# Stages 2 to 4 of an attention and two-layer kernel in five blocks of 924 tokens, not six of 768

## The chip, the core and the metric

The kernel runs on one NeuronCore of a Trainium2 chip. TensorE does the matrix products, VectorE and ScalarE prepare operands and take results away, GpSimd (POOL) helps in the first stage, and every transfer between HBM and SBUF is issued by SyncE (SP), one queue in program order. The metric is the device time of one execution in microseconds; lower is better.

## The reference

Inputs are fp32. An attention through 32 memory slots (8 batches, 8 heads, 576 tokens, width 64) is followed by two layers over all 4608 tokens:

```
attn_out = _attn_ref(**attn_kwargs)                       # [8, 8, 576, 64]
x = attn_out.transpose(0, 2, 1, 3).reshape(4608, 512)
r = np.maximum(x @ w_in, 0.0)                             # moe:  512 -> 2048
x = (s * (r * r) + b) @ w_out                             #       2048 -> 512
h = x @ w_in2                                             # moe2: 512 -> 2048
g = h * (1.0 / (1.0 + np.exp(-1.702 * h)))
y = g @ w_out2                                            #       2048 -> 512
```

## The kernel before

There are four stages. Stage 1 is the attention with `w_in` and the relu, batch by batch; it writes `r` to HBM. Stage 2 is `r*r @ w_out` (weights `wo`), stage 3 `x @ w_in2` with its gating (`w1`), stage 4 `g @ w_out2` (`w2`). Between stages the data go through HBM (`r`, `x`, `g`).

**Blocks and products.** Stages 2 to 4 go over the tokens in `N` = 6 blocks of 2 x `TS` = 768. Each block's product is done in the manner of Strassen with seven half-size products instead of eight, numbered 1 to 7, on sums and differences of the halves of the operands; the tokens are halved too, so a matmul has `TS` = 384 columns. Each operand is split into a high part (`oh`) and a low part (`ol`) that the fast fp32 format holds, and each product of operands is three matmuls: high by high, high by low, low by high (lines 885 to 887 and 1013 to 1015). One product on one quarter of the 2048-wide dimension is a group of 12 matmuls, and a block has 7 x 4 = 28 groups. PSUM tiles `X`, `Y` and `Z` collect them.

**Preparing operands.** `down` (stages 2 and 4) loads for each quarter five tiles `A`, `B`, `D`, `C`, `E` (line 856); in stage 2 ScalarE squares them (line 858). Product 6 needs three subtractions on VectorE in a row, `A-B`, `D-B` and `D-A` (lines 865 to 867), then ScalarE (or VectorE) makes the high part (`hi`) and VectorE the low part (`lo`). `up` (stage 3) loads four `x` tiles per block and makes 14 operand tiles that are used by all four quarters. `leave` and `gate` take results out of PSUM and send them to HBM.

**Weights.** The weights of the seven products are prepared during the stage before (`prepare`) and written to HBM, each as high and low part side by side, 512 KB. `weights` loads 28 of them once at the start of a stage, where they stay. In stage 2 the quarters 0 to 2 are loaded as 256 KB and split at the start; quarter 3 (`kept`) is split in stage 1 and stays in SBUF.

**Slots.** SBUF tiles come from two pools of equal slots (line 192): 30 of 4 KB per partition for weights (`w`), 31 of 3 KB for everything else (`t`). A tile can be loaded when an earlier one of its pool has been read for the last time.

**The order.** Nothing is ordered by loops. Every step is recorded with a due time, the engines that can do it with an estimated cost, and what it reads and writes. `Order.sort` then takes one step after the other, by due time among those that can start, and hands out the slots of a pool in the order of due times. `B2` = 58.5 is the planned length of a block, from which all due times of stages 2 to 4 follow. The result is one fixed order per engine.

## Time and profile before

| | |
|---|---|
| median of the runs | 1363.14 us (1362.56 to 1363.47) |
| span of the profiled execution | 1361.4 us |
| TensorE busy (PE) | 1348.1 us, 99% |
| VectorE busy (DVE) | 1035.4 us, 76% |
| ScalarE busy (ACT) | 806.5 us, 59% |
| moved by DMA | 336.73 MB, mean 247 GB/s |

The profile gives the span from the first to the last instruction of one execution; its whole time is not given beside it, and the median of the runs lies 1.7 us above the span. Stage 1 takes the first 317 us; stages 2, 3 and 4 follow with borders near 658 and 996 us. Matmuls overlap one another, so their busy time is longer than the distance at which they start, and that distance is what counts. SP's column in order of time shows when a transfer was issued; the view of DMA issues shows how long it took to land.

### The profile page before, as it was taken

Reading aid. Unit: us, or ns where it says so; the run is one execution under the profiler, and the core shown is the slowest. Engines: PE = TensorE matmul, PEld = TensorE weight load, DVE = VectorE, ACT = ScalarE, POOL = GpSimd, SP = SyncE. Lnnn points to the kernel's source line nnn. Section 1 sums busy time; section 2 is a strip of 40 time slices with the busy share of each in tenths; the row PEclk is TensorE's granted clock in tenths of the full one; section 3 lists DMA queues with packets and bytes.
Section 4 is the critical chain, followed back from the end, with each engine's and each line's share of the span. In section 5 each row is a group of like instructions: output and inputs, shape, how many; then the busy total and the mean of one; then the engine's idle time right before and its main releaser. Section 6 shows DMA issues by size and latency. Waiting matters only on the chain.

```text
span 1361.4 us, 23704 instructions
## 1 busy us (share of the span) xinstructions
PE 1348.1 (99%) x9184; PEld 1306.9 (96%) x9184; DVE 1035.4 (76%) x1384; ACT 806.5 (59%) x1104; POOL 52.2 (4%) x42
## 2 busy tenths in 40 slices
PE   7999999999999999999999999999999999999998
PEld 5798888899999999999999999999999999999998
DVE  6878996899988898998756856665376776968682
ACT  5766666789777787777545554645443444434351
POOL 2201220200000000000000000000000000000000
PEclk8999999999999999999999999999999999999999
DMA  9989999797755775599876666576996544355541
GB/s 365 366 295 349 364 344 327 260 325 245 277 185 174 235 259 162 193 362 339 314 274 248 248 237 228 209 259 238 315 339 212 183 162 163 128 174 160 196 131 48
DMA packets 126400, 336.73 MB, mean 247 GB/s; under 512 B 14288, under 2 KB 14544, under 8 KB 126288
## 3 DMA queue, kind: packets, MB, share of 16 engines
q1 hardware_dynamic: 126288, 335.22, 70.6%
q8 instruction: 72, 1.18, 0.4%
q14 instruction: 40, 0.33, 0.1%
HBM read 205.93 MB, written 129.24 MB: 246 GB/s over the span
## 4 chain that ended last, share of the span: by engine, by line
PE 94%; DVE 4%; DMA 2%; issue 0%; ACT 0%; SPq 0%; ACTq 0%
PE X L885 10%; PE X L886 10%; PE X L887 10%; PE Y L885 5%; PE X L1014 5%; PE X L1015 5%; PE Y L886 5%; PE X L1013 5%; PE Y L887 5%; PE h L294 4%; PE h L296 4%; PE h L295 4%; PE Y L1014 2%; PE Y L1015 2%; PE Y L1013 2%; PE Z L885 2%
## 5 line engine op out<-in xcount | busy, mean ns | idle before, releaser
L294 PE MATMUL h<-ah,mh 128*128 128x288 f32 x512 | 155.3, 303 | 0.2
L270 DVE TENSOR_TENSOR u<-Y,u 128x768 f32<-128x768 f32 x60 | 57.4, 957 | 125.6 <-ACT u L1021 56.0
L296 PE MATMUL h<-ah,ml 128*128 128x288 f32 x512 | 151.4, 296 | 0.1
L295 PE MATMUL h<-al,mh 128*128 128x288 f32 x512 | 150.9, 295 | 0.0
L885 PE MATMUL X<-oh,wo 128*128 128x384 f32 x384 | 128.5, 335 | 0.0
L887 PE MATMUL X<-oh,wo 128*128 128x384 f32 x384 | 128.5, 335 | 0.0
L886 PE MATMUL X<-ol,wo 128*128 128x384 f32 x384 | 128.5, 335 | 0.0
L1013 PE MATMUL X<-oh,w 128*128 128x384 f32 x384 | 128.4, 334 | 0.0
L885 PE MATMUL X<-oh,w 128*128 128x384 f32 x384 | 128.4, 334 | 0.0
L1015 PE MATMUL X<-oh,w 128*128 128x384 f32 x384 | 128.4, 334 | 0.0
L886 PE MATMUL X<-ol,w 128*128 128x384 f32 x384 | 128.4, 334 | 0.0
L887 PE MATMUL X<-oh,w 128*128 128x384 f32 x384 | 128.4, 334 | 0.0
L1014 PE MATMUL X<-ol,w 128*128 128x384 f32 x384 | 128.4, 334 | 0.0
L791 ACT ACTIVATE r<-h 128x576 f32<-128x576 f32 x126 | 88.7, 705 | 61.6 <-PE h L296 45.8
L264 ACT CAST oh<-C 128x768 fp32r<-128x768 f32 x93 | 79.9, 868 | 76.2 <-PE X L887 25.3
L294 PEld LDWEIGHTS h<-ah,mh 128*128 128x128 f32 x512 | 96.2, 188 | 13.7 <-issue 6.6
L270 DVE TENSOR_TENSOR ol<-C,oh 128x768 fp32r<-128x768 f32 x96 | 91.0, 956 | 21.5 <-ACT oh L264 5.7
L270 DVE TENSOR_TENSOR ol<-A,oh 128x768 fp32r<-128x768 f32 x96 | 90.3, 955 | 10.6 <-PE X L886 6.0
L296 PEld LDWEIGHTS h<-ah,ml 128*128 128x128 f32 x512 | 96.1, 188 | 0.5 <-DVE ml L270 0.4
L295 PEld LDWEIGHTS h<-al,mh 128*128 128x128 f32 x512 | 96.3, 188 | 0.0
L270 DVE TENSOR_TENSOR ol<-E,oh 128x768 fp32r<-128x768 f32 x48 | 45.6, 956 | 49.9 <-PE X L887 15.9
L264 ACT CAST oh<-A 128x768 fp32r<-128x768 f32 x79 | 67.9, 877 | 23.8 <-PE Y L886 8.1
(219 smaller groups left out, 3640.2 us busy)
## 6 DMA issues: line engine op xcount, KB each, us to landing
w<-w SPq DMA_DIRECT2D x112, 512.0 KB, 5.5
r<-r SPq DMA_DIRECT2D x128, 288.0 KB, 4.4
kv<-in_kv SPq DMA_DIRECT2D x72, 258.0 KB, 5.3
g<-u SPq DMA_DIRECT2D x48, 384.0 KB, 3.2
raw<-in_w SPq DMA_DIRECT2D x32, 512.0 KB, 4.9
q<-in_q SPq DMA_DIRECT2D x32, 288.0 KB, 5.5
A<-r SPq DMA_DIRECT2D x24, 384.0 KB, 5.0
B<-r SPq DMA_DIRECT2D x24, 384.0 KB, 5.1
```

The source lines that it names most:

```text
L264: self.order.add(due, [self.act(n, lambda: nc.scalar.copy(out(), src()), psum), self.dve(n, lambda: nc.vector.tensor_copy(out(), src()), f ...
L270: self.order.add(due, [self.dve(n, lambda: nc.vector.tensor_tensor(out(), a(), b(), op=op), port=port)], r, w, first)
L294: self.nc.tensor.matmul(ps, wh, xh, start=start and i == 0, stop=False)
L295: self.nc.tensor.matmul(ps, wh, xl, start=False, stop=False)
L296: self.nc.tensor.matmul(ps, wl, xh, start=False, stop=(i == n - 1))
L791: self.act(2 * HS, lambda: nc.scalar.activation(self.pairs(self.two(r, n=HS)), T[h][:, :, 0:HS], AF.Relu), psum=True),
L885: nc.tensor.matmul(out, T[w][:, 0, c], T[h][:, p], start=f, stop=False, skip_group_check=True)
L886: nc.tensor.matmul(out, T[w][:, 0, c], T[l][:, p], start=False, stop=False, skip_group_check=True)
L887: nc.tensor.matmul(out, T[w][:, 1, c], T[h][:, p], start=False, stop=last, skip_group_check=True)
L1013: nc.tensor.matmul(out, T[w][:, 0, c], T[h][:, k], start=f, stop=False, skip_group_check=True)
L1014: nc.tensor.matmul(out, T[w][:, 0, c], T[l][:, k], start=False, stop=False, skip_group_check=True)
L1015: nc.tensor.matmul(out, T[w][:, 1, c], T[h][:, k], start=False, stop=k == 1, skip_group_check=True)
```

## The change

The token blocks become five: four of 924 tokens and one of 912, so `TS` is 462 or 456. `B2` becomes 70.2, which keeps the planned length of a stage at 351 (6 x 58.5 = 5 x 70.2). The two pools become one of 53 slots of 4 KB per partition (`m`). With weights and operands in one pool, 12 weights no longer stay: those of products 7 and 5 of `wo` and of product 7 of `w2`. They are loaded for every block (`STREAM`), for `wo` from a copy with both parts that is written to HBM first (`both`). The output tensor gets the tokens as its last dimension, since the blocks differ in length.

```diff
-    BUFS = {"w": 30, "t": 31, "ps": 4, "km": 2, "an": 3, "nm": 4, "sm": 4}
+    BUFS = {"m": 53, "ps": 4, "km": 2, "an": 3, "nm": 4, "sm": 4}
+    HOME = {"w": "m", "t": "m"}
...
-    B1, B2 = 38.5, 58.5
+    B1, B2 = 38.5, 70.2
-    TS, N = 384, 6
+    TSS = (462, 462, 462, 462, 456)
+    N = len(TSS)
+    STREAM = {("wo", 7), ("wo", 5), ("w2", 7)}
...
+            elif (name, i) in self.STREAM:
+                self.both(d + 1, name, i, q, o)
...
-    def weights(self, name, i, q, due):
+    def weights(self, name, i, q, due, s=0):
...
+        o = ("w", (name, i, q, 1, s) if s else (name, i, q, 1))
+        if (name, i, q) in self.whole and not s:
...
+            if (name, i) in self.STREAM:
+                self.both(due + 4, name, i, q, o)
             return
+        again = name == "wo"
+        at = (name, i, q, "b") if again else (name, i, q)
...
+    def both(self, due, name, i, q, o):
+        self.dma(due, lambda: self.dram(name, i, q, "b", cols=1024), lambda: self.T[o].bitcast(F32).rearrange("p a b -> p (a b)"),
+                 ((*o, "h"), (*o, "l")), ((name, i, q, "b"),), 512)
...
-                w = ("w", (name, i, q) if (name, i, q) in self.kept else (name, i, q, 1))
+                w = ("w", (name, i, q, 1))
+                if (name, i) in self.STREAM and s:
+                    w = ("w", (name, i, q, 1, s))
+                    self.weights(name, i, q, d - 9, s)
+                elif (name, i, q) in self.kept:
+                    w = ("w", (name, i, q))
```

Every step of stages 2 to 4 is planned anew. Three places show how.

VectorE at the start of stage 2's second block (`D`, `B`, `A` are the loaded tiles of that block, one set per quarter; `ol` the low parts, those made from `D` belong to product 6). Before:

```order
L270 TENSOR_TENSOR ol_896_5028<-D_872_4855,oh_894_5022 128x768
L270 TENSOR_TENSOR D_881_4901<-D_881_4901,A_812_4490 128x768
L270 TENSOR_TENSOR A_822_4540<-B_886_4940,A_822_4540 128x768
L270 TENSOR_TENSOR A_826_4562<-B_890_4964,A_826_4562 128x768
L270 TENSOR_TENSOR ol_900_5067<-D_881_4901,oh_898_5048 128x768
L270 TENSOR_TENSOR B_886_4940<-D_888_4947,B_886_4940 128x768
L270 TENSOR_TENSOR B_890_4964<-D_891_4967,B_890_4964 128x768
L270 TENSOR_TENSOR D_888_4947<-D_888_4947,A_822_4540 128x768
L270 TENSOR_TENSOR D_891_4967<-D_891_4967,A_826_4562 128x768
L270 TENSOR_TENSOR ol_906_5109<-B_868_4832,oh_893_5007 128x768
L270 TENSOR_TENSOR ol_909_5115<-B_878_4895,oh_897_5030 128x768
L270 TENSOR_TENSOR ol_913_5134<-D_888_4947,oh_908_5113 128x768
```

After:

```order
L282 TENSOR_TENSOR ol_898_5065<-D_877_4926,oh_897_5059 128x924
L282 TENSOR_TENSOR D_882_4955<-D_882_4955,A_830_4638 128x924
L282 TENSOR_TENSOR B_887_4980<-D_889_4997,B_887_4980 128x924
L282 TENSOR_TENSOR A_832_4663<-B_891_5003,A_832_4663 128x924
L282 TENSOR_TENSOR D_889_4997<-D_889_4997,A_831_4657 128x924
L282 TENSOR_TENSOR ol_906_5110<-D_882_4955,oh_903_5103 128x924
L282 TENSOR_TENSOR B_891_5003<-D_892_5018,B_891_5003 128x924
L282 TENSOR_TENSOR ol_908_5129<-D_889_4997,oh_907_5112 128x924
L282 TENSOR_TENSOR D_892_5018<-D_892_5018,A_832_4663 128x924
L282 TENSOR_TENSOR ol_913_5152<-B_873_4905,oh_894_5038 128x924
L282 TENSOR_TENSOR ol_915_5156<-B_878_4930,oh_899_5079 128x924
L282 TENSOR_TENSOR ol_917_5160<-D_892_5018,oh_914_5154 128x924
```

Between the low parts of product 6 for the first and the second quarter there are three other instructions before and four after; on TensorE a group of product 3 stood between the two quarters before, and none after.

SP in stage 2, the same block's end and the next one's loads (`wo_7_0_b` is the HBM copy of product 7, quarter 0, of `wo`; `x_..` are results on their way out, `w1_..` the next stage's weights). Before:

```order
L259 DMA x_1_0_0_5561<-a_865_4823 128x768
L259 DMA x_1_1_0_5618<-u2_933_5228 128x768
L259 DMA A_990_5636<-r_0_0_485 128x768
L259 DMA A_994_5658<-r_1_0_522 128x768
L259 DMA A_998_5679<-r_2_0_604 128x768
L259 DMA raw_1001_5703<-in_w1 128x1024
L259 DMA A_1005_5724<-r_3_0_645 128x768
L259 DMA C_1007_5742<-r_0_1_784 128x768
L259 DMA x_1_0_1_5748<-c12_1000_5699 128x768
L259 DMA raw_1012_5766<-in_w1 128x1024
L259 DMA C_1015_5774<-r_1_1_870 128x768
L259 DMA C_1018_5794<-r_2_1_966 128x768
```

After:

```order
L271 DMA x_1_0_0_5594<-a_861_4831 128x924
L271 DMA wo_994_5630<-wo_7_0_b_4402 128x1024
L271 DMA wo_996_5648<-wo_7_1_b_4444 128x1024
L271 DMA wo_1000_5684<-wo_7_2_b_4468 128x1024
L271 DMA x_1_1_0_5690<-u2_930_5223 128x924
L271 DMA wo_1003_5707<-wo_7_3_b_3970 128x1024
L271 DMA w1_1_1_5713<-w1_993_5614 128x1024
L271 DMA wo_1008_5748<-wo_5_0_b_4493 128x1024
L271 DMA w1_2_1_5756<-w1_998_5655 128x1024
L271 DMA x_1_0_1_5761<-c12_1005_5728 128x924
L271 DMA wo_1016_5780<-wo_5_1_b_4516 128x1024
L271 DMA w1_4_1_5796<-w1_1002_5705 128x1024
```

The loads of streamed weights now stand between the stores of results and the loads of the next block's `A`.

SP in stage 3, where the second block's `x` tiles are loaded (`x00` to `x11`; `g_..` are results on their way out). Before:

```order
L259 DMA x00_1388_8107<-x_1_0_0_5561 128x768
L259 DMA w1_5_3_8123<-w1_1376_8009 128x1024
L259 DMA x10_1392_8141<-x_1_1_0_5618 128x768
L259 DMA g_0_0_1_1_8144<-u4_1384_8085 128x768
L259 DMA g_0_0_0_1_8161<-g_1389_8121 128x768
L259 DMA w1_1395_8166<-w1_5_3_8123 128x1024
L259 DMA g_0_0_1_0_8186<-u2_1380_8047 128x768
L259 DMA x01_1400_8190<-x_1_0_1_5748 128x768
L259 DMA g_0_1_0_0_8204<-a_1387_8104 128x768
L259 DMA w1_7_3_8219<-w1_1377_8026 128x1024
L259 DMA x11_1403_8224<-x_1_1_1_5425 128x768
```

After:

```order
L271 DMA x00_1346_7756<-x_1_0_0_5594 128x924
L271 DMA w1_3_3_7759<-w1_1337_7665 128x1024
L271 DMA w1_1348_7775<-w1_7_3_7737 128x1024
L271 DMA g_0_1_1_1_7791<-u4_1344_7735 128x924
L271 DMA g_0_1_0_1_7794<-g_1347_7773 128x924
L271 DMA w1_1350_7809<-w1_6_3_7740 128x1024
L271 DMA w1_1351_7812<-w1_3_3_7759 128x1024
L271 DMA g_0_1_1_0_7829<-u2_1341_7702 128x924
L271 DMA x10_1354_7831<-x_1_1_0_5690 128x924
L271 DMA g_0_2_0_0_7845<-a_1345_7754 128x924
L271 DMA x01_1358_7864<-x_1_0_1_5761 128x924
L271 DMA x11_1360_7869<-x_1_1_1_5441 128x924
```

Before, two of the four loads stood ahead of the stores of the first block's quarter 0 shown here and two behind them; after, they stand one quarter later, the last two behind the first store of quarter 2.

## Rows read from the trace of the kernel before

**Rows 1.** The page's head and its engine shares (busy us, share of the span, instructions).

```profile
span 1361.4 us, 23704 instructions
...
PE 1348.1 (99%) x9184; PEld 1306.9 (96%) x9184; DVE 1035.4 (76%) x1384; ACT 806.5 (59%) x1104; POOL 52.2 (4%) x42
```

**Rows 2.** Windows of stages 2, 3 and 4: length, busy us by engine, PEclk, DMA share, GB/s.

```profile
317.00:658.00 341.00, 341.00 (x1968) 340.68 (x1968) 304.03 (x389) 267.69 (x361) 0.00 (x0) 1.00 0.72 246
658.00:996.00 338.00, 338.00 (x1951) 338.00 (x1951) 202.37 (x284) 173.91 (x232) 0.00 (x0) 1.00 0.71 258
996.00:1357.00 361.00, 361.00 (x2084) 361.00 (x2084) 262.11 (x294) 147.94 (x182) 0.00 (x0) 1.00 0.51 170
```

**Rows 3.** TensorE's waits, first and last of six: line, releaser: us, times, longest.

```profile
PE s L554 <- DMA kv<-in_kv: 3.1, 2, 1.5
...
PE x L641 <- ACT km L264: 0.5, 1, 0.5
```

**Rows 4.** Timeline of TensorE in stage 2: start us, us, engine, line, operation, tiles.

```profile
400.00 0.34 PE L887 MATMUL X<-oh,wo 128*128 128x384 f32 x1
...
429.99 0.34 PE L886 MATMUL X<-ol,wo 128*128 128x384 f32 x1
```

**Rows 5.** Timeline of TensorE in stage 1.

```profile
206.96 0.29 PE L295 MATMUL h<-al,mh 128*128 128x288 f32 x1
...
216.24 0.29 PE L296 MATMUL h<-ah,ml 128*128 128x288 f32 x1
```

**Rows 6.** Groups by line and shape: count | busy us, mean ns | idle before, releasers.

```profile
L270 DVE TENSOR_TENSOR ol<-C,oh 128x768 fp32r<-128x768 f32 x96 | 91.0, 956 | 21.5 <-ACT oh L264 5.7 <-PE X L887 2.8 <-PE Y L886 2.6
...
L264 ACT CAST oh<-C 128x768 fp32r<-128x768 f32 x93 | 79.9, 868 | 76.2 <-PE X L887 25.3 <-PE X L886 19.3 <-DVE C L270 10.8
...
L270 DVE TENSOR_TENSOR w<-cw,w 128x512 fp32r<-128x512 f32 x32 | 21.9, 686 | 5.8 <-ACT w L264 5.7
...
L264 ACT CAST w<-cw 128x512 fp32r<-128x512 f32 x28 | 17.2, 618 | 2.1 <-DVE cw L336 2.0
```

**Rows 7.** Timeline of VectorE at the start of stage 2's second block.

```profile
371.50 0.95 DVE L270 TENSOR_TENSOR D<-D,A 128x768 f32<-128x768 f32 x1
...
378.44 1.82 DVE L270 TENSOR_TENSOR ol<-B,oh 128x768 fp32r<-128x768 f32 x2
380.18 1.82 DVE L270 TENSOR_TENSOR ol<-D,oh 128x768 fp32r<-128x768 f32 x2
...
383.66 5.30 DVE L270 TENSOR_TENSOR ol<-A,oh 128x768 fp32r<-128x768 f32 x6
```

**Rows 8.** Timeline of TensorE at the same place.

```profile
373.83 0.34 PE L886 MATMUL X<-ol,wo 128*128 128x384 f32 x1
...
380.07 0.34 PE L886 MATMUL Y<-ol,wo 128*128 128x384 f32 x1
...
382.15 0.34 PE L886 MATMUL X<-ol,wo 128*128 128x384 f32 x1
```

**Rows 9.** Windows of 40 us, columns as in rows 2.

```profile
120.00:160.00 40.00, 40.00 (x476) 34.23 (x475) 34.79 (x54) 27.62 (x45) 9.91 (x8) 1.00 1.01 363
...
600.00:640.00 40.00, 40.00 (x232) 39.76 (x231) 34.98 (x42) 29.88 (x39) 0.00 (x0) 1.00 0.94 344
640.00:680.00 40.00, 40.00 (x232) 40.00 (x231) 31.24 (x47) 21.95 (x32) 0.00 (x0) 1.00 0.89 329
```

**Rows 10.** DMA issues by tiles: count, KB each, median us to landing.

```profile
w<-w SPq DMA_DIRECT2D x112, 512.0 KB, 5.5
...
A<-r SPq DMA_DIRECT2D x24, 384.0 KB, 5.0
...
raw<-in_wi SPq DMA_DIRECT2D x16, 512.0 KB, 7.9
```

**Rows 11.** Timeline at the end of the span.

```profile
1357.95 0.56 DVE L270 TENSOR_TENSOR a<-Z,a 128x384 f32<-128x384 f32 x1 [2.56 <-PE Z L899]
```

More of the change, by code (lines that the diff above doesn't have):

```diff
@@ L41, with __init__, of @@
     WEIGHT = {"dve": 2.0, "pool": 1.6, "act": 1.0}
-    def __init__(self, bufs):
-        self.bufs, self.ops, self.rank, self.fill, self.until, self.since = bufs, [], [], None, 0, 0
+    def __init__(self, bufs, home):
+        self.bufs, self.home = bufs, home
+        self.ops, self.rank, self.fill, self.until, self.since = [], [], None, 0, 0
         self.narrow = set()
         self.wrote, self.read, self.users = {}, {}, {}
+    def of(self, k):
+        return self.home.get(k[0], k[0])
     def add(self, due, ways, r=(), w=(), first=0):
@@ L100, in sort @@
                     ok = True
-                    for tag in {x[0] for x in new}:
-                        mine = [x for x in new if x[0] == tag]
+                    for tag in {self.of(x) for x in new}:
+                        mine = [x for x in new if self.of(x) == tag]
                         f = free[tag]
@@ L158, in sort @@
                 if not uses[x]:
-                    heapq.heappush(free[x[0]], last[x] + 0.2)
+                    heapq.heappush(free[self.of(x)], last[x] + 0.2)
         self.span = max(end)
@@ L209, in __init__ @@
         self.T = {}
-        self.order = Order(self.BUFS)
+        self.order = Order(self.BUFS, self.HOME)
         self.d = {}
@@ L217, in t @@
         pool = self.ps if k[0] == "ps" else self.sb
-        x = pool.tile(shape, dt, tag=k[0], bufs=self.BUFS[k[0]], name=f"{self.name(k)}_{self.n}")
+        tag = self.HOME.get(k[0], k[0])
+        x = pool.tile(shape, dt, tag=tag, bufs=self.BUFS[tag], name=f"{self.name(k)}_{self.n}")
         self.T[k] = x
@@ L223, in name, with two @@
         return k[1][0] if isinstance(k[1], tuple) and isinstance(k[1][0], str) else k[0]
-    def two(self, k, dt=F32, n=TS):
+    def two(self, k, n, dt=F32):
         return self.t(k, [P, 2, n], dt)
@@ L799, in pairs, with out @@
         return x.rearrange("p a b -> p (a b)").rearrange("p (t a) -> p a t", a=2)
+    def out(self, s, i, j):
+        t = 2 * sum(self.TSS[:s]) + self.TSS[s] * j
+        return self.a["out"][i][:, :, t:t + self.TSS[s]]
     def rows(self, i, j, t, n):
@@ L811, in x, with minus @@
             return self.pairs(T[src]) if key[0] == "wo" else T[src]
[L813 to L814 removed]
+        self.hi(due, n, lambda: self.two(h, n // 2, F32R), x, (src,), (h,))
+        self.lo(due + 0.4, n, lambda: self.two(l, n // 2, F32R), x, lambda: T[h], (src, h), (l,))
         return h, l
[L817 removed]
+    def minus(self, due, n, out, a, b, new=False):
         T = self.T
[L820 removed]
+        self.tt(due, n, (lambda: self.two(out, n // 2)) if new else (lambda: T[out]), lambda: T[a], lambda: T[b], ALU.subtract,
                 [k for k in (a, b) if k != out], (out,))
     def load(self, due, k, name, s, i, j, half):
+        TS = self.TSS[s]
         if name != "r":
             at = (name, s, i, j, half) if name == "g" else (name, s, j, half)
[L827 removed]
+            self.dma(due, lambda: self.two(k, TS).rearrange("p a b -> p (a b)"), lambda: self.dram(*at, cols=2 * TS), (at,), (k,), TS)
             return
[L829 to L831 removed]
+        t = 2 * sum(self.TSS[:s]) + TS * half
+        us = range(t // self.HS, -(-(t + TS) // self.HS))
+        self.dma(due, lambda: self.two(k, TS).rearrange("p a b -> p (a b)"), lambda: self.rows(i, j, t, TS), [("r", i, j, u) for u in us], (k,), TS)
     def down(self, name, src, s, due):
[L835 removed]
+        nc, T, TS = self.nc, self.T, self.TSS[s]
         pas = self.B2 / 7
@@ L925, in copy @@
             if not scaled:
-                self.on_act(due, n, lambda: nc.scalar.copy(self.two(k), T[X][:, :, 0:TS]), (X,), (k,), first, psum=True)
+                self.on_act(due, n, lambda: nc.scalar.copy(self.two(k, TS), T[X][:, :, 0:TS]), (X,), (k,), first, psum=True)
                 return
```

69 lines of the change are left out of this document (29 added, 40 removed).

## The prediction

> **What bounds the kernel now.** I read the page's engine shares first, then the windows of the three stages that the change touches, then who TensorE waits for, then single matmuls in order of time. TensorE is busy 99% of a span of 1361.4 us [rows 1]. In each of stages 2, 3 and 4 it is busy for the whole window at a granted clock of 1.00, which is the 2.4 GHz level, while VectorE is busy 304 of 341 us in stage 2, 202 of 338 in stage 3 and 262 of 361 in stage 4 [rows 2]. TensorE's list of waits has six entries of 9.4 us together, the longest 3.1 us and the last 0.5 us, and all belong to stage 1 (lines 232 to 769) [rows 3]. So behind the first stage nothing waits in front of TensorE, and only what TensorE itself does there can shorten the kernel.
>
> What one matmul costs is read from start to start, since they overlap. In stage 2 there are 173 steps from 400.00 to 429.99 us: 29.99 / 173 = 173.35 ns for 384 columns [rows 4]. At 2.4 GHz the columns alone take 384 / 2.4 = 160.0 ns, so each matmul costs 13.35 ns beyond its columns. In stage 1 there are 70 steps from 206.96 to 216.24 us: 132.57 ns for 288 columns, 12.57 ns beyond 120.0 [rows 5].
>
> **The change, part by part.**
>
> *Fewer, wider matmuls.* Stages 2 to 4 have 28 groups of 12 matmuls per block: 3 x 6 x 336 = 6048 before, 3 x 5 x 336 = 5040 after, of which 4032 have 462 columns and 1008 have 456. The columns stay the same (6048 x 384 = 4032 x 462 + 1008 x 456 = 2,322,432), so only the cost beyond the columns can fall. If it is 13.35 ns for each matmul at any width, 462 columns take 192.5 + 13.35 = 205.85 ns and 456 take 203.35: 829.99 + 204.98 = 1034.96 us against 6048 x 173.35 = 1048.42, so 13.46 us less. If instead it grows a little with width, as a straight line through the two measured widths says (40.78 ns for 96 columns, 0.4248 ns each), they take 206.48 and 203.93 ns: 1038.1 us, 10.3 less. I take 13.46, by the row that is nearest (the same lines, the same operands), and keep 10.3 as the other end. All of it lies on the path, since TensorE never stops there.
>
> TensorE's rows show 13.35 ns beyond the columns [rows 4]. The Trainium skill, on its page "TensorE: Matmul & The Clock Gate", section "Wait — 56ns, not 53.3ns?", gives a fixed cost of about 2.5 ns for a warm matmul that follows another, measured on bf16. By that the 1008 matmuls saved would be worth 2.5 us and not 13.5; the trace of this kernel, with its split fp32 operands and a weight load for every matmul, does not agree, and the row decides.
>
> *Work on VectorE and ScalarE.* Each operation on an operand gets 924 columns and not 768, and there are five sixths as many. VectorE's subtraction takes 686 ns at 512 columns and 956 at 768, so 1.055 ns a column and 1.12 us at 924; ScalarE's cast takes 618 and 868, so 1.02 us at 924 [rows 6]. Stage 2 has 44 such subtractions per block: 264 x 0.956 = 252.4 us become 220 x 1.12 = 246.4. VectorE so loses 6 us of 304 while the stage loses 4.5 of 341; its share stays near 89%. This is hidden behind TensorE before and after; its price if the cover goes is in the next item.
>
> *The order at the start of a block of stage 2.* This is the one place where I expect a new wait. In the trace of before, TensorE takes the low part of the first quarter of product 6 at 373.83 us and that of the second quarter two groups later, because a group of product 3 of the block before stands between them. After the change the two quarters follow each other directly, and on VectorE five instructions now lead from one low part to the next (four before), three of them subtractions for later quarters. In a burst VectorE does one 768-column operation per (5.30 - 0.95) / 5 = 0.87 us [rows 7], so about 0.87 + 156 x 0.001055 = 1.035 us at 924. Five take 5.17 us; TensorE comes back after 12 x 0.20585 = 2.47. The second low part is thus 2.7 us late, less the lead that the first one has. Before, that lead was about 2.3 us (VectorE has gone on to the next row at 371.50, TensorE needs it at 373.83), and two groups later only 0.7 and 1.0 us (378.44 + 0.96 against 380.07; 380.18 + 0.96 against 382.15) [rows 7, 8]. So the cost is 0 to 2.7 us, 0.4 with the lead of before; I take 1.2, since the later leads are small.
>
> *Transfers for the three streamed products.* Stage 2 gets 8 stores and 32 loads of 512 KB, 21.0 MB (two of the stores fall into stage 1); stage 4 gets 16 loads, 8.4 MB. Stage 2 moves 246 GB/s x 341 us = 83.9 MB now, so 104.9 MB in some 336 us: 312 GB/s, and the DMA share goes from 0.72 to about 0.91. Between 120 and 160 us the share is 1.01 and TensorE is busy for 40.00 of 40 us [rows 9], so a full DMA side alone does not stop it. In stage 2's last third the shares are 0.94 and 0.89 [rows 9] and would be 1.13 and 1.08: some 8 us of transfers slide later, and what slides there are loads and stores of the next stage's weights, of which the last quarter is used more than 40 us into stage 3. I take 0, and 0 to 3 us for the range.
>
> *Fewer slots.* 61 become 53 for both kinds of tile. Following the waits in both built orders, I counted for each load how many matmuls lie between the last one that must end before it can be issued (for its slot, or for what stands ahead of it on SP) and the one that first needs the data. Before, the smallest count was 73, for C in stage 4: 73 x 173.35 = 12.7 us, and TensorE never waited. After, the smallest are 73 for A and for the streamed weights in stage 2 (15.0 us at 205.85 ns), 85 for other weights (17.5 us), 145 for the x tiles of stage 3 (29.8 us, 193 before). What must fit: a load lands in 5.0 to 5.5 us, and in 7.9 us at the longest median that the trace has [rows 10]; A then needs a square and a cast of about 1.02 us each and a subtraction of 1.12. That is 11.1 us with the slowest landing, under 15.0. Cost 0; 0 to 2 us for the range.
>
> *The end.* The last half product is added in 0.56 us at 384 columns [rows 11]; 72 more columns cost 72 x 1.055 ns = 0.08 us, and 36 KB more in the last store at (5.5 - 5.0) us for 128 KB [rows 10] 0.14. I take 0.1 together, 0 to 0.5.
>
> **Sum.** On the span of 1361.4 us: -13.46 + 1.2 + 0.1 = 1349.2. The profiled execution's own time is not given beside its span; the median of the runs, 1363.14, lies 1.7 us above the span, and I carry that over: 1363.14 - 12.16 = **1351.0 us**. Its own bounds: 1363.14 - 13.46, less 0.6 for the fastest of the runs, gives 1349.0; with the line through two widths and the upper ends (2.7 at the block start, 0.5 at the end) 1356.0.
>
> **The rivals.**
>
> *1. VectorE's burst is late at every block.* For it: VectorE's 89% of stage 2, and leads of 0.7 and 1.0 us. Against it: TensorE waits nowhere now, and the product of operation length and count falls. Price: 2.7 us at each of stage 2's four later block starts, 10.8 us, gives 1360.6; at half of it 1355. I set this case at 1357.
>
> *2. Stage 3 runs out of slots; slower than before.* 28 weights are resident, so 25 slots are left where there were 33. The 14 operand tiles of a block are held until its last quarter; the other 11 must hold four x tiles, a difference, the outputs on their way out and the preparation of the next weights. If the preparation sits on them, the next block's x tiles are loaded too late, and with all of it in the open each of the four later starts waits for landing, cast and subtraction, 7.9 + 1.02 + 1.12 = 10.0 us: 1363.1 - 13.4 + 40 = 1390. It decides from (13.4 + 2.7) / 4 = 4.0 us per start on; at half of the full price the time is 1370. Against it: the 145 matmuls, 29.8 us.
>
> *3. The cost beyond the columns is not paid per matmul.* If it were in proportion to the columns (0.0348 ns each), 462 would take 208.6 ns, nothing would be saved, and the 1.3 us added would give 1364.4: no change. Against it: 288 columns would then take 130.0 ns, and 132.57 are measured [rows 5].
>
> *4. Width counts in steps.* 288 and 384 are multiples of 32, 462 and 456 are not; no row has such a width with these operands. If each were charged as 480, a matmul would take 213.35 ns and the stages 1075.3 us, so 1391: slower. Nothing in the trace speaks for it.
>
> That the change doesn't do what it says is excluded: the built order has 5040 wide matmuls.
>
> **How the numbers follow.** Forecast 0.70; rival 1 0.15; rival 2 0.05; rival 3 0.07; rival 4 0.03. A measurement of this kernel can tell about 0.2%, 2.7 us. Faster by more than that: 0.70 + 0.13 = 0.83. Within it: 0.07 and the far end of rival 1, 0.02, so 0.09. Slower: 0.08. The range takes the forecast's bounds and most of rival 1: 1349 to 1358.
>
> **What would show it.** Right: from start to start 205.9 ns at 462 columns (206.5 by the line, 208.6 by rival 3, 213.4 by rival 4); TensorE's list of waits behind stage 1 has one or two entries of 1 to 3 us in stage 2 on a subtraction that makes ol, and none on a load; stage 3's windows show it busy throughout; stage 2's DMA share is near 0.9. Wrong: waits on A, wo, x or w loads, or a gap at each block start, would mean that slots or transfers, not the matmul count, set the time.

## The result and the profile after

| | before | after |
|---|---|---|
| median of the runs, us | 1362.94 (1362.56 to 1363.47) | 1373.02 (1370.52 to 1375.08) |
| span of the profiled execution, us | 1361.4 | 1373.3 (run of 1375.08) |
| mean DMA rate over the span, GB/s | 247 | 266 |

The changed kernel is slower: ratio 1.0073 (95% interval 1.0058 to 1.0087), 10.1 us. The forecast was 1351.0 us, faster, with a range of 1349 to 1358, so the side was missed, and the time lies 22.0 us above the forecast and 15.0 us above the range.

The engine shares answer [rows 1]: TensorE is again busy 99% of the span, and its weight loads (PEld) are less busy.

```profile
span 1373.3 us, 21368 instructions
PE 1359.5 (99%) x8176; PEld 1210.1 (88%) x8176; DVE 1013.5 (74%) x1253; ACT 797.1 (58%) x995; POOL 51.6 (4%) x42
```

The windows of the three stages, cut at their new borders, answer [rows 2]: TensorE's busy time fills stage 3 and lacks 0.7 us in stage 2 and 0.3 in stage 4, at a granted clock of 1.00 throughout. The DMA share of stage 2 rose from 0.72 to 0.85.

```profile
core 0: us, PE busy (x) PEld busy (x) DVE busy (x) ACT busy (x) POOL busy (x), PEclk, DMA share, GB/s
317.00:661.00 344.00, 343.33 (x1640) 307.41 (x1639) 302.76 (x348) 259.87 (x308) 0.00 (x0) 1.00 0.85 294
661.00:1002.00 341.00, 341.00 (x1627) 306.17 (x1626) 205.60 (x266) 177.90 (x215) 0.00 (x0) 1.00 0.71 255
1002.00:1370.00 368.00, 367.70 (x1758) 330.68 (x1756) 244.58 (x232) 147.80 (x158) 0.00 (x0) 1.00 0.59 200
```

TensorE's list of waits answers [rows 3] (us in total, how often, the longest). Behind stage 1 there is one entry, on the subtraction that makes `ol`; there is none on a load, on the streamed weights or on a slot.

```profile
PE s L577 <- DMA kv<-in_kv: 3.1, 2, 1.5
PE vw L792 <- ACT mh L276: 1.8, 1, 1.8
...
PE X L920 <- DVE ol L282: 0.7, 1, 0.7
```

So the lost time is not in waits. It is in the distance at which matmuls start, read as in [rows 4]: the first and the last row of TensorE's timeline of the changed kernel between 400 and 430 us (stage 2, 143 steps), 1100 and 1130 us (stage 4, 143 steps) and 1320 and 1350 us (the last block, 456 columns, 146 steps).

```profile
399.64 0.37 PE L921 MATMUL X<-oh,wo 128*128 128x462 f32 x1
...
429.99 0.37 PE L920 MATMUL Z<-ol,wo 128*128 128x462 f32 x1
...
1099.76 0.37 PE L919 MATMUL X<-oh,w 128*128 128x462 f32 x1
...
1129.79 0.37 PE L921 MATMUL X<-oh,w 128*128 128x462 f32 x1
...
1319.72 0.37 PE L921 MATMUL Y<-oh,w 128*128 128x456 f32 x1
...
1349.90 0.36 PE L920 MATMUL X<-ol,w 128*128 128x456 f32 x1
```

30.35 / 143 = 212.2 ns, 30.03 / 143 = 210.0 ns and 30.18 / 146 = 206.7 ns, where 205.85 and 203.35 were forecast. Over all steps of a stage the means at 462 columns are 211.6, 210.6 and 210.0 ns in stages 2, 3 and 4, and 206.6 to 206.7 at 456. Beyond its columns (192.5 and 190.0 ns) a matmul now costs 17.5 to 19.1 and 16.7 ns, where 384 columns cost 13.35. Single steps vary: 203 to 222 ns at 462 columns and 199 to 214 at 456, in a pattern that repeats with every group of 12 matmuls, where before nearly all steps were 172 to 175.

### The profile page after: what moved, and what is told of

It reads as the page before. It is cut to its first block, busy times and chain, and to the rows that moved or that the text cites. A ratio compares the mean times of both kernels' runs of the same rounds, so it can differ in the third digit from the quotient of the medians.

```text
span 1373.3 us, 21368 instructions
## 1 busy us (share of the span) xinstructions
PE 1359.5 (99%) x8176; PEld 1210.1 (88%) x8176; DVE 1013.5 (74%) x1253; ACT 797.1 (58%) x995; POOL 51.6 (4%) x42
## 3 DMA queue, kind: packets, MB, share of 16 engines
q8 instruction: 64, 1.05, 0.3%
## 4 chain that ended last, share of the span: by engine, by line
PE 96%; DMA 2%; DVE 1%; ACT 1%; issue 0%; SPq 0%; ACTq 0%
PE X L919 10%; PE X L921 10%; PE X L920 10%; PE h L306 5%; PE X L1047 5%; PE Y L919 5%; PE Y L921 5%; PE X L1049 5%; PE Y L920 5%; PE X L1048 5%; PE h L308 5%; PE h L307 5%; PE Y L1047 2%; PE Y L1049 2%; PE Y L1048 2%; PE Z L919 2%
## 5 line engine op out<-in xcount | busy, mean ns | idle before, releaser
L282 DVE TENSOR_TENSOR u<-Y,u 128x924 f32<-128x924 f32 (+1 forms) x50 | 55.8, 1117 | 101.6 <-ACT u L1055 46.2
L920 PE MATMUL X<-ol,wo 128*128 128x462 f32 (+1 forms) x320 | 119.5, 373 | 0.7 <-DVE ol L282 0.7
L919 PE MATMUL X<-oh,w 128*128 128x462 f32 (+1 forms) x320 | 119.6, 374 | 0.0
L1047 PE MATMUL X<-oh,w 128*128 128x462 f32 (+1 forms) x320 | 119.4, 373 | 0.0
L921 PE MATMUL X<-oh,wo 128*128 128x462 f32 (+1 forms) x320 | 119.4, 373 | 0.0
L919 PE MATMUL X<-oh,wo 128*128 128x462 f32 (+1 forms) x320 | 119.3, 373 | 0.0
L1049 PE MATMUL X<-oh,w 128*128 128x462 f32 (+1 forms) x320 | 118.9, 372 | 0.0
L1048 PE MATMUL X<-ol,w 128*128 128x462 f32 (+1 forms) x320 | 118.7, 371 | 0.0
L921 PE MATMUL X<-oh,w 128*128 128x462 f32 (+1 forms) x320 | 118.7, 371 | 0.0
L920 PE MATMUL X<-ol,w 128*128 128x462 f32 (+1 forms) x320 | 118.4, 370 | 0.0
L282 DVE TENSOR_TENSOR ol<-A,oh 128x924 fp32r<-128x924 f32 (+1 forms) x80 | 88.0, 1116 | 30.0 <-ACT oh L276 12.4
L276 ACT CAST oh<-C 128x924 fp32r<-128x924 f32 (+1 forms) x74 | 73.0, 1002 | 53.9 <-PE X L920 14.2
L282 DVE TENSOR_TENSOR ol<-C,oh 128x924 fp32r<-128x924 f32 (+1 forms) x80 | 88.0, 1116 | 16.2 <-PE X L920 4.8
L276 ACT CAST oh<-A 128x924 fp32r<-128x924 f32 (+1 forms) x73 | 72.5, 1009 | 30.5 <-PE Y L921 11.0
L282 DVE TENSOR_TENSOR ol<-E,oh 128x924 fp32r<-128x924 f32 (+1 forms) x40 | 44.1, 1117 | 58.2 <-PE X L920 23.2
```

The costliest lines, as they stand in the source:

```text
L276: self.order.add(due, [self.act(n, lambda: nc.scalar.copy(out(), src()), psum), self.dve(n, lambda: nc.vector.tensor_copy(out(), src()), f ...
L282: self.order.add(due, [self.dve(n, lambda: nc.vector.tensor_tensor(out(), a(), b(), op=op), port=port)], r, w, first)
L919: nc.tensor.matmul(out, T[w][:, 0, c], T[h][:, p], start=f, stop=False, skip_group_check=True)
L920: nc.tensor.matmul(out, T[w][:, 0, c], T[l][:, p], start=False, stop=False, skip_group_check=True)
L921: nc.tensor.matmul(out, T[w][:, 1, c], T[h][:, p], start=False, stop=last, skip_group_check=True)
L1047: nc.tensor.matmul(out, T[w][:, 0, c], T[h][:, k], start=f, stop=False, skip_group_check=True)
```

## Experiments

Three theories stood at the start. **A**: a matmul pays for a width or a start place that is not a multiple of some unit. **B**: the cost simply grows with width above 384. **C**: the other engines, the transfers or the place of the slots slow TensorE down.

### Widths with TensorE alone

A kernel of matmuls only, in the three-product pattern (high by high, high by low, low by high), weights of two tiles in turn, no engine beside it, 96 matmuls for each width:

```
for n in PACKED:
    x = ps.tile([P, 2, 512], F32, tag="ps", bufs=2, name=f"n{n}")
    for g in range(8):
        group(x, n, n, ws[g % 2], g == 0)      # 12 matmuls; halves at columns 0 and n
```

> The disputed cost by itself: nothing but groups of 12 matmuls as in stages 2 to 4 (two weight tiles, split fp32 operands), 96 of each width from 288 to 512 columns, with no other engine and no transfer beside them; the second half of the operand stands right behind the first (start at 4 x columns bytes), and at the end four widths once more with the halves 2048 bytes apart. It leaves the whole computation of the reference out. Theory A (width or start that is no multiple of a granule costs): 13.3 ns beyond the columns at 288, 320, 352, 384, 416, 448, 480, 512 and perhaps 400, 432, 464, 496; about 17.5 ns at 456, 460, 462; and 13.3 at 462 again where the halves are 2048 bytes apart, if it is the start and not the width. Theory B (the cost grows with the width from somewhere above 384 on): 13.3 ns up to 384 or so, then rising smoothly past 17 at 462 to more at 512, granule or not, apart halves or not. Theory C (the other engines, the transfers or the place of the tiles in SBUF slow TensorE): 13.3 ns at every width here.

TensorE's timeline, first and last row of two stretches: 480 columns (69 steps) and 512 columns (66 steps).

```profile
284.80 0.38 PE L40 MATMUL n<-ol,w 128*128 128x480 f32 x1
...
299.87 0.38 PE L40 MATMUL n<-ol,w 128*128 128x480 f32 x1
...
370.81 0.39 PE L40 MATMUL n<-ol,w 128*128 128x512 f32 x1
...
385.77 0.39 PE L40 MATMUL n<-ol,w 128*128 128x512 f32 x1
```

480 columns start every 15.07 / 69 = 218.4 ns, 18.4 beyond the columns; 512 columns every 14.96 / 66 = 226.7 ns, 13.3 beyond. The other widths, as the mean from start to start in the steady part of each stretch, less columns / 2.4:

```
columns   288   320   352   384   400   416   432   448   456   462   464   480   496   504   512
beyond   13.3  13.3  12.2  13.3  16.1  15.5  13.4  20.0  16.6  17.6  16.6  18.3  17.8  18.9  13.3   ns
```

462 and 456 columns cost here, with TensorE alone, what they cost in stage 4 of the changed kernel, so C falls for the bulk of this cost; for the 0.6 and 1.6 ns that stages 3 and 2 lie higher it stays open. B falls with 512. A in its simple form falls too: 448 and 480 are multiples of 32 and among the dearest. 288, 320, 384 and 512 have a steady step; the dear widths (but for 448) have a ragged one. Where the second half begins counts too: with the halves 2048 bytes apart, at the end of the run, 456, 462, 464 and 488 columns cost 18.9, 19.2, 15.6 and 16.7 ns, against 16.6, 17.6, 16.6 and 20.0 with the halves one behind the other; 462 does not fall to 13.3. The two rows of front matter that the forecast rested on, 384 and 288 columns [rows 4, 5], are both of the cheap kind.

### 464 and 480 columns in the kernel

```diff
-    TSS = (462, 462, 462, 462, 456)
+    TSS = (464, 464, 464, 464, 448)
```

> The changed kernel with blocks of 928, 928, 928, 928 and 896 tokens: 464 and 448 columns, both multiples of 16, all else the same. Theory A: 464/2.4 + 13.35 = 206.7 ns and 200.0 ns, so 4032 x 206.7 + 1008 x 200.0 = 1035.0 us in stages 2 to 4 against about 5040 x 210.1 = 1058.9 in the changed kernel: 1373 - 24 = 1349 us. Theory B: about 211 and 204 ns, no gain: 1373 us. Theory C: as B, 1373 us.

1365.26 us (1361.09 to 1366.95), ratio 1.001 (1.0001 to 1.002). The step is 210.0 ns at 464 and 202.7 at 448 columns; alone 464 had shown the same 210.0, but 448 had 206.7. The price is again in the step, and the only loss in a wait is some 0.1 us.

```diff
-    TSS = (462, 462, 462, 462, 456)
+    TSS = (480, 480, 480, 480, 384)
```

> The changed kernel with four blocks of 480 columns and one of 384, multiples of 32. Theory A: 200.0 + 13.35 = 213.35 ns and 173.35 ns: 4032 x 213.35 + 1008 x 173.35 = 1035.0 us, total 1349 us. Theory B: 480 columns at 18 ns or more beyond the columns, 218 ns, and 173.35 for the last block: 1053.7 us, total 1368 us. Theory C: about 217.5 and 177.5 ns, 1055.9 us, 1370 us.

1370.68 us (1370.23 to 1371.53), ratio 1.0058 (1.0041 to 1.0075). The step is 218.3 ns at 480, as alone, and 173.5 at 384; one wait costs 1.1 us. Multiples of 32 by themselves gain nothing.

### Six blocks of 384 with the change's pool and streamed weights

```diff
-    B1, B2 = 38.5, 70.2
-    TSS = (462, 462, 462, 462, 456)
+    B1, B2 = 38.5, 58.5
+    TSS = (384,) * 6
```

> The changed kernel with six blocks of 384 columns again (planned block length 58.5), but with its one pool of 53 slots of 4 KB and its three streamed products. Theories A and B: 173.35 ns as before, so 1363 us, plus at most 3 us where VectorE is late in stage 2. Theory C (one pool, all tiles at the same place of a 4 KB slot, more transfers): 384 columns take 4 ns more too, some 177.5 ns, so 1363 + 6048 x 0.004 = 1388 us.

1373.41 us (1372.44 to 1374.49), ratio 1.0076 (1.0061 to 1.0091): as slow as the change, for another reason. The step is 173.35 ns, as before; here TensorE waits. Its list of waits, those behind stage 1:

```profile
PE X L920 <- DVE ol L282: 3.7, 1, 3.7
...
PE X L1047 <- ACT u L1055: 2.1, 2, 1.2
...
PE Y L920 <- DVE ol L282: 1.3, 1, 1.3
```

The longest, at the start of stage 2's second block, in VectorE's timeline and then in TensorE's:

```profile
342.17 0.41 DVE L342 TENSOR_SCALAR cw<-cw 128x512 uint32<-128x512 uint32 x1
345.01 1.02 DVE L975 SCALAR_TENSOR_TENSOR u<-Y,sc,u 128x768 f32<-128x768 f32 x1 [2.43 <-ACT u L966]
...
348.69 2.69 DVE L282 TENSOR_TENSOR ol<-A,oh 128x768 fp32r<-128x768 f32 x3
```

```profile
345.63 0.34 PE L919 MATMUL X<-oh,wo 128*128 128x384 f32 x1
349.70 0.44 PE L920 MATMUL X<-ol,wo 128*128 128x384 f32 x1 [3.73 <-DVE ol L282]
...
351.28 0.52 PE L919 MATMUL X<-oh,wo 128*128 128x384 f32 x1
351.60 0.52 PE L920 MATMUL X<-ol,wo 128*128 128x384 f32 x1
```

VectorE stands 2.43 us behind ScalarE's `u`, then does five steps on weights before the `ol` that TensorE needs. ScalarE's `u` itself had stood 4.18 us behind a product of TensorE, as its row says (two halves merged in one row):

```profile
343.75 1.23 ACT L966 ACTIVATE u<-X,bw,sc 128x384 f32<-128x384 f32 x2 [4.18 <-PE X L921]
```

The high part to which this `ol` belongs was there already (TensorE's matmul at 345.63 reads it), so it is the fixed order of VectorE's steps, with `u` ahead of the `ol`, that makes it late, more than VectorE's speed. After TensorE's wait of 3.73 us the next matmuls run on at 173 ns for 1.6 us; then ten steps of 320 ns follow, which is 384 columns at the 1.2 GHz level (the granted clock of the window from 350 to 356 us is 0.72). The steps longer than usual add up to 9.7 us over the kernel, 5.6 of them here, and the rest of the 10.5 us lies in stage 1. So with six blocks of 384 the change's pool and streams bring waits; at 462 the only wait behind stage 1 costs 1.1 us.

### One weight slice, one operand, one output

The widths run again, with further widths, and then with everything but the width held still:

```
for n in (384, 448, 462, 480, 512):
    x = ps.tile([P, 2, 512], F32, tag="ps", bufs=2, name=f"one{n}")
    for g in range(96):
        nc.tensor.matmul(x[:, 0, 0:n], ws[0][:, 0, 0:128], h[:, 0:n], ...)
```

> The kernel's whole computation is left out; TensorE multiplies alone, with no other engine beside it, so its time is not compared. Three parts. First, the three-product pattern of the kernel at widths not yet seen (256, 272, 304, 336, 360, 368, 376, 392, 408, 424 columns). Second, at 384, 448, 462, 480 and 512 columns, 96 matmuls on one and the same 128 weight columns, one operand and one half of the accumulator, then the same with the weights changed at every matmul. Third, 384 columns from operand places that shift, and pairs of unequal widths in turn (462 and 306, 480 and 288, 512 and 256). Theory D (the cost beyond the columns is set by the width of a matmul alone): every width shows its own cost whatever weights, operand place or accumulator half it uses, 13.3 ns at 384 and 512, 20 at 448, 17.6 at 462, 18.3 at 480; shifted places leave 384 at 173.3 ns; a pair shows the sum of its two costs (for 462 and 306 some 31 ns beyond 768 / 2.4 = 320 ns). Theory W (it comes from the change of weights or from where operands and sums lie): on one weight slice and one place all five widths fall to one constant, and only the changing weights bring back 17 to 20 ns; the 384 columns from shifting places rise above 173.3. Theory M (it is a matter of widths that are multiples of 32 or 64, with exceptions at 352, 448 and 480 from the weight change): 256 shows 13.3, 272, 304, 336 and 368 show more than that, and 448 and 480 fall to 13.3 on one weight slice.

384, 448, 462, 480 and 512 columns cost 13.3, 20.0, 19.2, 16.7 and 13.3 ns beyond the columns, to 0.02 ns the same with one weight slice and with two in turn; TensorE's timeline groups the 480 matmuls of either part, and both last equally long:

```profile
164.98 99.56 PE L51 MATMUL one<-oh,w 128*128 128x384 f32 x480
264.38 99.56 PE L56 MATMUL two<-oh,w 128*128 128x384 f32 x480
```

So a change of weights has no part in it, and W falls as far as that goes. A weight load still stood before each matmul in both parts (480 loads for 480 matmuls), and no run here leaves it out. But 384 columns whose operand starts at a different column each time rise to 16.8 ns: the place counts, against D. Of the new widths 256 shows 13.1 ns; 272, 304 and 336 show 11.1 to 12.3, below 13.3, and 376 to 424 between 14.5 and 16.7, so M's multiples of 32 are no rule either.

The pairs of two widths in turn do not show the sum of their costs. 512 with 256 columns costs 26.7 ns a pair, which is twice 13.3, but 480 with 288 also costs 26.7, where 16.7 and 13.3 would make 30.0, and 462 with 306 costs 28.9, where D expected some 31. So the cost is not a property of one matmul alone. In these pairs the half of the output changes from matmul to matmul as well as the width, and no further run told the two apart.

### Widths that showed 13.3 ns, in the kernel

```diff
-    TSS = (462, 462, 462, 462, 456)
+    TSS = (512, 512, 512, 512, 256)
```

> The changed kernel with blocks of 1024, 1024, 1024, 1024 and 512 tokens (matmuls of 512 columns, in the last block 256) in place of 924 and 912; nothing else differs. If the width alone made the change slower (512 columns showed 13.3 ns beyond the columns with TensorE alone), 4032 matmuls start every 226.7 ns and 1008 every 120 ns, together 1034.9 us for stages 2 to 4 against 1057 in the changed kernel: 1351 us, 0.9% faster than the kernel before, less what the short last block loses by waiting (its weights are made in 39 us instead of 70: bound 0 to 10 us by the 384-column blocks, which lost some 10). If instead a wide matmul beside the other engines always costs the 17 to 18 ns of 462 and 480, the pitch is 231 ns and the time 1369 to 1373 us. If what the wide blocks cost is a wait on weights or slots, it shows as waits in stages 2 to 4, with pitch 226.7 all the same.

**1350.54 us** (1349.80 to 1351.10), ratio to the kernel before 0.9907 (0.9892 to 0.9921). TensorE's timeline from 430 to 460 us, 134 steps:

```profile
429.62 0.39 PE L921 MATMUL X<-oh,wo 128*128 128x512 f32 x1
...
460.00 0.39 PE L920 MATMUL X<-ol,wo 128*128 128x512 f32 x1
```

30.38 / 134 = 226.7 ns; at 256 columns the mean is 119.9. TensorE's waits behind stage 1 are gone (0.1 us in one step). This is the change as it stands, with other five numbers, 22.5 us faster than with 462: these numbers alone made it slower. They set the width, and with it the column at which the second half of an operand begins (462 or 512). It also beats both kernels, at the time that the forecast had named.

```diff
-    TSS = (462, 462, 462, 462, 456)
+    TSS = (512, 512, 512, 384, 384)
```

> The changed kernel with blocks of 1024, 1024, 1024, 768 and 768 tokens (512 and 384 columns a matmul, the two wide widths that showed 13.3 ns beyond the columns); nothing else differs. By the width alone: 3024 matmuls every 226.7 ns and 2016 every 173.3 ns, 1034.9 us: 1351 us, and less waiting in the last block than with 512 tokens. If wide matmuls in the kernel always cost 17 to 18 ns: 231 and 173.3, about 1365 us. If the blocks of 384 wait as in the kernel with six such blocks on one pool: up to 5 us more than 1351.

1353.67 us (1352.79 to 1354.71), ratio 0.993 (0.9915 to 0.9945): 3.1 us above the last one. TensorE's list of waits has one entry behind stage 1, at 610 us, in the last block of stage 2, the second of 384 columns; the profiled execution also reached stage 2 1.3 us later.

```profile
PE Y L920 <- DVE ol L282: 2.1, 1, 2.1
```

```diff
-    TSS = (462, 462, 462, 462, 456)
+    TSS = (384, 512, 512, 512, 384)
```

> The same five widths in another order: blocks of 768, 1024, 1024, 1024 and 768 tokens. The matmuls are the same in number and width as in the kernel with 512, 512, 512, 384, 384 columns less one place; so by the width alone the sum is the same 1034.9 us and the time 1351 us. What differs is where the burst of VectorE at the start of stage 2's second block falls: after a first block of 384 columns it has 58 us instead of 76 or 71. If that burst is what made six blocks of 384 on one pool wait 3.7 us at 345.6 us and lose the clock after it, this kernel loses 3 to 7 us there and stands at 1354 to 1358; if not, both orders give the same time within 1 us.

1359.77 us (1358.72 to 1360.18), ratio 0.9973 (0.9963 to 0.9984), 6.1 above the other order of the same widths. TensorE's list of waits and its timeline at the start of stage 2's second block:

```profile
PE X L920 <- DVE ol L282: 4.2, 2, 3.3
...
PE Y L1047 <- ACT g L1071: 1.4, 1, 1.4
```

```profile
342.98 0.40 PE L919 MATMUL X<-oh,wo 128*128 128x512 f32 x1
346.65 0.58 PE L920 MATMUL X<-ol,wo 128*128 128x512 f32 x1 [3.28 <-DVE ol L282]
347.03 0.63 PE L921 MATMUL X<-oh,wo 128*128 128x512 f32 x1
347.46 0.63 PE L919 MATMUL X<-oh,wo 128*128 128x512 f32 x1
```

A first block of 384 columns brings back the wait of six such blocks and the lower clock after it; behind a first block of 462 or 512 columns no wait of stage 2's second block costs more than 1.1 us. That a longer block gives VectorE the time fits this; it was not tested by itself. The steps longer than usual sum to 8.0 us here, 2.4 with 384 last, 0.1 with 512 and 256.

### The place of the operand

48 matmuls each of five widths, from nine start columns, one weight slice:

> The kernel's whole computation is left out; TensorE multiplies alone, so its time is not compared. 48 matmuls each of 384, 448, 462, 480 and 512 columns on one weight slice, with the operand taken from column 0, 2, 4, 8, 16, 32, 48, 64 or 128 on. Theory D1 (the width alone counts, and the 3.4 ns more that 384 columns showed from shifting places came from the change of place between neighbours): each width keeps one pitch for all nine places, 173.3, 206.7, 211.7, 216.7 and 226.7 ns. Theory D2 (the place counts too): 384 and 512 columns leave 173.3 and 226.7 when they begin off a multiple of 16 columns (64 bytes), by 2 to 5 ns, and 448 or 480 may fall to 200 or 213.3 from some place.

```
from column     0     2     4     8    16    32    48    64   128
384          (*)   13.3  15.6  13.3  13.3  16.0  14.6  13.3  13.3
448          20.0  20.1  13.3  17.8  13.3  17.2  15.6  20.0  20.0
462          19.2  14.1  14.2  14.2  19.1  14.2  14.2  19.2  19.2
480          16.8  13.3  16.8  17.8  18.3  17.8  16.0  16.8  16.8
512          13.4  20.0  18.4  20.0  15.5  18.9  20.1  13.6  13.3   ns beyond the columns
(*) the first stretch, in which the clock was still rising
```

TensorE's timeline in four windows of 8.5 us; each row is start, length of the group, and its number of matmuls: 462 columns from column 0 and from 2, 512 columns from 0 and from 2.

```profile
175.17 9.04 PE L37 MATMUL n462from<-oh,w 128*128 128x462 f32 x42
...
185.30 9.05 PE L37 MATMUL n462from<-oh,w 128*128 128x462 f32 x43
...
359.16 9.02 PE L37 MATMUL n512from<-oh,w 128*128 128x512 f32 x39
...
370.34 9.03 PE L37 MATMUL n512from<-oh,w 128*128 128x512 f32 x38
```

Less the length of the last matmul (0.37 and 0.39 us), these are 8.67 / 41 = 211.5 and 8.68 / 42 = 206.7 ns at 462, and 8.63 / 38 = 227.1 and 8.64 / 37 = 233.5 ns at 512. D2 holds in that the place counts, and a multiple of 16 columns is not enough: 384 and 512 lose 2.7 and 5.5 ns from column 32. From columns 0, 64 and 128 each width costs the same within 0.3 ns, which fits a place counted within 64 columns (256 bytes); other multiples of 64 were not run. 13.3 ns is the least of the table, and each of these widths but 462 reaches it from some place.

A second run took the kernel's own pattern, with the two halves one behind the other:

```
m = slice(f + n * p, f + n * p + n)     # p: half 0 or 1; n = 462 or 456; f = 0, 2, ... 62
```

> The kernel's whole computation is left out; TensorE multiplies alone, so its time is not compared. The kernel's three-product pattern at 462 and 456 columns, where the first half of the operand begins at column f of its slot (f = 0, 2, ... 62) and the second half right behind it at f + 462 or f + 456. If the cost follows from width and place (place counted from a 64-column, 256-byte, boundary), f = 0 shows the 210.1 and 206.6 ns of the first widths run, and some other f brings 462 columns down to about 206.7 ns, which single matmuls showed from columns 2, 4, 8, 32 and 48; 456 columns have a place with 203.3. The pattern of two halves then has the mean of its two places. If place counts only where one operand is read again and again, all 32 places show 210.1 and 206.6.

462 columns lie between 206.6 (f = 6) and 212.3 ns (f = 58); f = 0, the place of the changed kernel, has 210.1. 456 columns lie between 205.6 (f = 44) and 211.1 (f = 30), with 206.6 and 206.7 at f = 0 and f = 6; the 203.3 that was expected at some place does not show. The stretch with f = 6 in TensorE's timeline from 74 to 92 us, 88 steps of 18.18 / 88 = 206.6 ns:

```profile
73.77 0.37 PE L40 MATMUL n462from<-ol,w 128*128 128x462 f32 x1
...
91.95 0.37 PE L41 MATMUL n462from<-oh,w 128*128 128x462 f32 x1
```

### The same width at another place, in the kernel

The changed kernel, its operand tiles 24 bytes further on in their slots; blocks, widths and steps are the change's.

```diff
     def two(self, k, n, dt=F32):
+        if dt == F32R:
+            x = self.t(k, [P, 1024], dt)
+            self.T[k] = x[:, 6:6 + 2 * n].rearrange("p (a b) -> p a b", a=2)
+            return self.T[k]
         return self.t(k, [P, 2, n], dt)
```

> The changed kernel, same widths (462 and 456), same order; only the operand tiles of stages 2 to 4 begin at column 6 of their slot, not at column 0, so the halves lie at columns 6 and 468 (6 and 462 in the last block). If place within 64 columns counts in the kernel as it does with TensorE alone, where 462 columns went from 210.0 to 206.7 ns and 456 stayed at 206.6, a 462-column matmul falls from the 210.0 to 211.6 ns of the changed kernel to 206.7 to 208 and 4032 of them save 11 to 16 us: 1357 to 1362 us, about the time of the kernel before. If place counts only with TensorE alone (in the kernel the mix of operands and the other engines' traffic set the cost), it takes 1373 us and the pitch stays. By either it is slower than the kernel with 512 columns, 1350.5 us.

1358.37 us (1357.79 to 1358.63), ratio to the kernel before 0.9966 (0.9953 to 0.9978), and 14.7 us below the change. TensorE's timeline from 400 to 430 us, 146 steps:

```profile
399.70 0.37 PE L925 MATMUL X<-oh,wo 128*128 128x462 f32 x1
...
429.87 0.37 PE L924 MATMUL Z<-ol,wo 128*128 128x462 f32 x1
```

30.17 / 146 = 206.6 ns, against 212.2 in the same window of the change; over the three stages the means are 206.7 to 206.9. 24 bytes turn the change from slower to faster, without a wait more or less: the one in stage 2 is still 0.7 us. The profiled spans differ by 17.3 us: 4032 x (210.7 - 206.8) = 15.7 us lie in the step, and 1.7 us in stage 1, before the first wide matmul.

### One pool, all weights kept, 384 columns

The edit is against the kernel of six blocks of 384 above.

```diff
     TSS = (384,) * 6
-    STREAM = {("wo", 7), ("wo", 5), ("w2", 7)}
+    STREAM = set()
```

> Six blocks of 768 tokens as before (384 columns), one pool of 53 slots as in the change, but the weights of all seven products stay, none is loaded per block. It stands between the kernel before and the one with six blocks, one pool and streamed weights (1373.4 us, with 3.7 us of waiting at 345.6 us, nine matmuls at the lower clock after it and 5 us of waits in stage 3). If the streamed weights (their loads, copies and the steps they put ahead of others) cause those waits, this kernel has none of them: 1363 us, ratio 1.00. If the single pool does (fewer slots, and the order that they give), the waits stay and it takes 1370 us or more; with 28 weights always held and 25 slots left for operands it may then even be slower than 1373.

1390.05 us (1387.86 to 1393.10), ratio 1.0205 (1.0188 to 1.0222). TensorE's list of waits, behind stage 1:

```profile
PE Y L920 <- DVE ol L282: 11.7, 8, 2.3
...
PE X L1047 <- ACT u L1055: 2.3, 2, 1.4
PE Z L920 <- DVE ol L282: 1.9, 4, 0.7
PE X L920 <- DVE ol L282: 1.7, 4, 0.7
```

The streams are not the cause of the 384-column waits as a whole; they relieve them, by 16.6 us. With 28 weights always held, 25 slots are left for everything else. The steps longer than usual sum to 24.9 us, 2.3 to 3.6 at each of four block starts in stage 4. It is not so at every place: at the start of stage 2's second block the streamed kernel lost 5.6 and 1.6 us and this one 3.0 and 2.0, so there the streams may cost some 2 us. That the slots are what makes `ol` late fits this, but only the sum was measured, and the chain from a slot to `ol` was not tested by itself.

## Why the prediction was wrong

**The step that failed** is the first and largest: "If it is 13.35 ns for each matmul at any width". It was taken from two widths, 384 and 288 [rows 4, 5], and the upper bound was the straight line through the same two, 206.5 ns. Both are cheap widths, from the places that they had. At 462 and 456 columns the cost was 18.2 ns (the mean of the three stages) and 16.7, so 4032 x (210.7 - 205.85) + 1008 x (206.7 - 203.35) = 19.6 + 3.4 = 23.0 us were missing. In place of -13.46 the term is +9.5. With the wait of 1.1 that gives 10.6 us; the medians differ by 10.1, the profiled spans by 11.9 (the profiled run is the slowest of the four), of which 1.3 lie in stage 1, before the first wide matmul.

**The rest of that step holds.** The columns do stay the same and only the count falls; TensorE's path has no slack. With five blocks of widths that cost 13.3 ns the same sum, 1034.9 us, came true: 1350.5 us measured for 1351.0 forecast. That the two agree so closely is in part luck, since the 1.2 us put down for a wait did not come there (0.1 us).

**Order at the start of a block of stage 2.** 1.2 us were taken, at the `ol` of the second quarter. That is where the only wait is; VectorE's timeline and then TensorE's (the step from 393.71 is 1.16 us and the next 0.31 in place of 0.21 each: 1.05 us lost):

```profile
388.00 1.12 DVE L282 TENSOR_TENSOR ol<-D,oh 128x924 fp32r<-128x924 f32 x1
...
392.13 1.12 DVE L282 TENSOR_TENSOR D<-D,A 128x924 f32<-128x924 f32 x1
393.69 1.12 DVE L282 TENSOR_TENSOR ol<-D,oh 128x924 fp32r<-128x924 f32 x1 [0.45 <-ACT oh L276]
```

```profile
393.71 0.48 PE L919 MATMUL X<-oh,wo 128*128 128x462 f32 x1
394.87 0.48 PE L920 MATMUL X<-ol,wo 128*128 128x462 f32 x1 [0.67 <-DVE ol L282]
395.18 0.37 PE L921 MATMUL X<-oh,wo 128*128 128x462 f32 x1
```

The operations came as estimated (a pitch of 1.03 us, 1.12 each); part of the delay is ScalarE's, whose cast VectorE waited 0.45 us for, which the forecast had left out. The later block starts lost nothing, so rival 1 did not come.

**Transfers and slots** were put at 0 and cost 0 at these widths: no wait on a load behind stage 1, stage 3 busy for the whole window (rival 2 did not come). Stage 2's DMA share was 0.85 at 294 GB/s, below the 0.91 and 312 forecast. The argument, that 15 us lie between a slot and its need, says nothing of the order on VectorE and ScalarE: with six short blocks the same pool cost 10 us with streams and 27 without, in waits on `ol` and `u` and none on a load. **The end** held: from the start of the last matmul to the end of the span it took 3.97 us for 3.85 before. The two items of that term, 0.08 and 0.14, add up to 0.22, not to the 0.1 taken. The 1363.14 from which the sum starts is the time of one of the four runs; their median is 1362.94. Neither changes the outcome.

**The rivals.** Rival 2 at half its price (1370 us) came nearest in time, but by chance: no wait of its kind shows. Rival 3 came nearest in the step (208.6 ns for 210.7), but its mechanism, a cost in proportion to the columns, is excluded by 512 columns at 13.3 ns. Rival 4 had the right kind of cause, a width that is not a friendly one, and was given 0.03 because "nothing in the trace speaks for it". Nothing in the trace spoke against it either: no row had such a width. Its form, charging 462 as 480, was wrong too, since 480 itself is dear.

The Trainium skill gives on "TensorE: Matmul & The Clock Gate", section "Wait — 56ns, not 53.3ns?", a fixed cost of about 2.5 ns for a warm matmul that follows another. At the upper clock no width here, from 256 to 512 columns, costs so little beyond its columns: the least is 11.1 ns, at 272, and these split fp32 operands have no one constant for all widths and places.

The same section of the Trainium skill says that at the lower clock the step is exactly columns / 1.2 GHz, with no constant. Here the traces agree: 320 ns for 384 columns and 426.7 ns for 512 after the two waits above.

## What to carry to other kernels

A kernel whose TensorE never waits can still lose time to a change that removes matmuls: read the step from start to start, not the busy share, and take a cost found at one width as no price for another before some 50 matmuls of the new width, operand type and start place have been run alone. For these operands 256, 288, 320, 384 and 512 columns were the cheap widths (13.1 to 13.3 ns) with the first half at the start of its slot and the second right behind it, and 272, 304, 336 and 352 cheaper still for each matmul (11.1 to 12.3); if the width is given, try where in its slot the operand begins. The order of block lengths counts too: the same five widths took 6.1 us more with a block of 384 columns first and one last than with both last.

## What the hardware showed that was not expected

- The cost of a matmul beyond its columns depends on width and on the operand's place within 64 columns, from 13.3 to 21.1 ns for 384 to 512 columns, whether or not the weights change, and with no other engine at work. In pairs of two widths in turn the costs do not add up. What in the chip does this is open; no run here looks inside. Why 462 columns cost 211.6 ns in stage 2 and 210.0 in stage 4 from the same places, and 448 columns 202.7 in the kernel and 206.7 alone, was not tried either.
- At the 1.2 GHz level it does not show: 426.7 ns for 512 columns is columns / 1.2 to the nanosecond, and 462 columns, dear at the upper level, take 385.1 ns there, where columns / 1.2 is 385.0 (13 steps from 9.975 to 14.981 us of the last run with TensorE alone, before its clock rose).
- Two of the kernels with ragged steps also scatter more from run to run: 4.6 us between the fastest and slowest of 462 columns and 5.9 at 464, against 0.9 to 2.7 for the kernel before, in groups of 4 to 13 runs, and 1.3 with 512 columns; with operands from column 6 the scatter was 0.8 us. It is no rule: 480 columns, ragged too, scattered by 1.3, and six steady blocks of 384 with all weights kept by 5.2. The cause was not tested.
